# A planned order instead of a hand-timed one: linear attention into a causal gated unit on one core

## The chip, the core and the metric

The kernel runs on one core of a Trainium2 chip. A core has a matrix engine (TensorE, PE in the profile; its weight loads are listed as PEld), VectorE (DVE), ScalarE (ACT), GpSimd (POOL) and SyncE (SP), which here only issues transfers. Each engine has its own queue of instructions; engines wait for each other by semaphores. The metric is the device time of one launch in microseconds. Before the change the median of three runs is 404.75 us (404.43 to 405.25). The profiled execution has a span of 405.2 us.

## What is computed

```python
# q, k, v: (8, 8, 576, 64): batch, heads, sequence, head width
kv  = einsum('bhsd,bhse->bhde', k, v)
out = einsum('bhsd,bhde->bhse', q, kv)
rms = sqrt(mean(out * out, axis=-1, keepdims=True) + 1e-06)
x   = out / rms * g_norm                  # then (B, H, S, D) -> (B, S, H*D) = (8, 576, 512)
gate_pre = sum over 5 taps of conv_w[tap] * x shifted causally by tap   # depthwise, along the sequence
gate = sigmoid(gate_pre)
val  = x @ w_val                          # w_val, w_out: (512, 512)
out  = (gate * val) @ w_out
```

The three weights of the second half (`w_val`, `conv_w`, `w_out`) arrive as 64-bit floats and are narrowed to 32 bits on the chip, in eight steps per 128-column or 128-row piece: five on VectorE and three on ScalarE.

## The kernel before

For each of the eight batches: `kv_product` (four calls, one for each pair of heads), `kv_copy`, `turn_q` (VectorE) or, in batches 0 and 1, `turn_q_rows` (TensorE, then copies on ScalarE), and then for five chunks of the sequence, last chunk first, the chain below. `ps("raw")` has two PSUM buffers, `ps("tp")` two, `ps("mm")` three.

```python
    def raw_product(b, c):     # TensorE: raw = q @ kv, 4 matmuls into "raw" ("mm" for some of batch 0)
    def square(b, c):          # ScalarE: sq = raw ** 2
    def sums(b, c, pair, n):   # VectorE: ss = sum over the head
    def powers(b, pair, m, n): # GpSimd: rt = ss ** -0.5; from batch 2 on mostly two chunks in one instruction
        nc.gpsimd.tensor_tensor(
            out=st["rts", b, pair][0:m, 0:n, :], in0=st["ss", b, pair][0:m, 0:n, :],
            in1=mhalf[0:m, 0:n, :], op=ALU.pow)
    def normalise(b, c):       # VectorE: x = raw * rt; frees the "raw" buffer
    def turn_x(b, c):          # TensorE: 4 transposes of x into "tp"
    def keep_x(b, c):          # ScalarE: xT = turned x * g
    def halo(b):               # GpSimd: 4 small copies, once for each batch
```

Then for each of four 128-column tiles `jt` the gate and the value, and after a batch's eight gated halves the output product:

```python
    def gate_start(b, jt):       # ScalarE: first tap
    def gate_tap(b, jt, tap):    # VectorE: four more taps, one instruction each
    def gate_end(b, jt):         # ScalarE: sigmoid
    def val_product(b, jt, n):   # TensorE: 4 matmuls of 128x288 into "mm"; n is the half of the sequence
    def gated(b, jt, n):         # VectorE: gv = val * gate; frees the "mm" buffer
    def out_product(i, c):       # TensorE: 4 matmuls of 128x512 into "mm"
    def store(i, c):             # ScalarE copies "mm" to SBUF, SyncE issues four transfers
```

The order in which all these steps go into the engines' queues is a plan by hand: each step is entered with a nominal time, and the steps are emitted sorted by it.

```python
    plan = []

    def at(when, step, *args):
        plan.append((when, len(plan), step, args))
    ...
    attention(0, 17.0, 1.9, 7.0, 14.0)
    narrow_all(("wval", 0), 16.0, 0.5)
    narrow_all(("wval", 1), 20.2, 1.0)
    gate(0, 0, 32.0, 0.8)
    ...
    products(0, begin, 3.4)
    attention(1, 41.0, 2.2, 34.0, 38.0)
    begin += NK * NV * 3.4
    for jt in range(NK):
        gate(1, jt, begin + 0.2 + 4.0 * jt, 0.8)
        at(16.0 + 2 * jt, stage_weight, "wout", jt)
        narrow_all(("wout", jt), begin + 1.0 + 4.6 * jt, 0.57)
    for b in range(1, B):
        products(b, begin, DV)
        begin += NK * NV * DV
        outputs(b - 1, begin)
        ...
            attention(b + 1, first, 3.0, first - 8.0, first - 7.0)
    outputs(B - 1, begin)

    with tc.manual_schedule():
        for _, _, step, args in sorted(plan, key=lambda p: p[0:2]):
            step(*args)
```

Of the kernel before, what the change touches and what calls it, by code (L numbers as in the profile page):

```python
# [15 lines left out]
P = 128  # L16
EPS = 1e-6


@with_exitstack  # L20
def kernel(
# [56 lines left out]
    def ps(kind, shape, name):  # L78
        return psum.tile(shape, FP32, tag=kind, bufs=BANKS[kind], name=name)

    plan = []

    def at(when, step, *args):
        plan.append((when, len(plan), step, args))
# [6 lines left out]
    mhalf = const.tile([P, 2, H], FP32, name="mhalf")  # L91
# [32 lines left out]
    def load_kv(b, i):  # L124

        for name, src in (("k", k), ("v", v)):
            t = loads.tile([P, H // 2, NJ, D], FP32, tag=f"{name}{i}", name=f"{name}{i}_{b}")
            nc.sync.dma_start(
                out=t[:].rearrange("p h j d -> p h (j d)"),
                in_=src[b, i * H // 2:(i + 1) * H // 2, 0:SF, :].rearrange(  # L130
                    "h (p j) d -> p h (j d)", j=NJ),
            )
            st[name, b, i] = t
        if i == 0:
            for n, src in enumerate((k, v)):
                nc.sync.dma_start(
                    out=tails[b % 2][n][0:T], in_=src[b, :, SF:S, :].rearrange("h s d -> s h d"))
# [15 lines left out]
    def load_q_rows(b):  # L153

        for i in range(3):
            t = loads.tile([P, NB, D], FP32, tag="q", bufs=4, name=f"q{b}_{i}")
            t = t[:].rearrange("p n d -> p (n d)")
            if i < 2:
                t = t[:, 0:H // 2 * NJ * D]
                nc.sync.dma_start(  # L160
                    out=t.rearrange("p (h a) -> p h a", h=H // 2),
                    in_=q[b, i * H // 2:(i + 1) * H // 2, 0:SF, :].rearrange(
                        "h (p j) d -> p h (j d)", j=NJ),
                )
                st["q", b, i] = t.rearrange("p (h j d) -> p h j d", h=H // 2, j=NJ)
            else:
                t = t[0:T, 0:C].rearrange("p (h d) -> p h d", h=H)
                nc.sync.dma_start(out=t, in_=q[b, :, SF:S, :].rearrange("h s d -> s h d"))
                st["q", b, i] = t
# [74 lines left out]
    def turn_cw():  # L244

        nc.vector.tensor_scalar_mul(gcol[:], gcol[:], math.sqrt(D))
        cwps = ps("tp", [P, K, NK], "cwps")
        nc.tensor.transpose(
            cwps[:].rearrange("p k o -> p (k o)"), cw[:], ident[0:NK * K, 0:NK * K])
        nc.vector.tensor_copy(cwT[:], cwps[:])  # L250
# [32 lines left out]
    def turn_q_rows(b, j):  # L283
# [3 lines left out]
        for hp in range(HP):  # L287
            for r in range(2):
                half, h = divmod(2 * hp + r, H // 2)
                nc.tensor.matmul(  # L290
                    pq[r * D:(r + 1) * D, hp, 0:m],
                    st["q", b, half][:, h, j, :] if j < NJ else st["q", b, 2][:, 2 * hp + r, :],
                    ident[0:m, 0:m], start=True, stop=True)
        to = new_qT(b)[:].rearrange("p h (n t) -> p h n t", t=TB)
# [41 lines left out]
    def sums(b, c, pair, n):  # L336
        m = size(c)
        if n == 0:
            for kind in ("ss", "rts"):
                st[kind, b, pair] = work.tile([P, 2, H], FP32, tag=kind, bufs=3, name=f"{kind}{b}_{pair}")  # L340
        nc.vector.reduce_sum(out=st["ss", b, pair][0:m, n, :], in_=st["sq", b, c][0:m], axis=AX.X)  # L341
        st["rt", b, c] = st["rts", b, pair][:, n, :]

    def powers(b, pair, m, n):
        nc.gpsimd.tensor_tensor(  # L345
            out=st["rts", b, pair][0:m, 0:n, :], in0=st["ss", b, pair][0:m, 0:n, :],
            in1=mhalf[0:m, 0:n, :], op=ALU.pow)
# [78 lines left out]
    def store(i, c):  # L426
        ot = work.tile([P, C], FP32, tag="ot", bufs=3, name=f"ot{i}_{c}")
        nc.scalar.copy(out=ot[:], in_=st["po", i, c][:])  # L428
        for j in range(HB):
            bb, n = divmod(c * HB + j, NB)  # L430
            nc.sync.dma_start(  # L431
                out=rows_out[2 * i + bb, n], in_=ot[j * TB:(j + 1) * TB, :])

    ORDER = [NJ] + list(range(NJ - 1, -1, -1))
    TAPS = range(K - 2, -1, -1)

    def attention(b, first, step, kv_first, turn_first):

        for hp in range(HP):
            at(kv_first + 1.5 * hp, kv_product, b, hp)  # L440
            if b >= TURNED:
                at(turn_first + 1.5 * hp, turn_q, b, hp)
        at(kv_first + 1.5 * HP, kv_copy, b)
        for n, c in enumerate(ORDER):
            if b < TURNED:
                at(turn_first + 0.6 * n, turn_q_rows, b, c)
                t, pair, member, members = first + n * step, n, 0, 1
            else:
                pair, member = divmod(n + 1, 2)
                t, members = first + (0.0, 3.0, 4.5, 9.5, 11.0)[n], 2 if n else 1  # L450
                member = member if n else 0
            at(t, raw_product, b, c)
            at(t + 0.8, square, b, c)
            at(t + 1.5, sums, b, c, pair, member)
            if member == members - 1:
                at(t + 1.6, powers, b, pair, size(c), members)
            t += 1.5 * (members - 1 - member)
            at(t + 4.5, normalise, b, c)
            at(t + 6.5, turn_x, b, c)
            at(t + 7.0, keep_x, b, c)  # L460
            if n == 1:
                at(t + 7.8, halo, b)

    gate_done = {}

    def gate(b, jt, t, step, tap_step=gate_tap):
        at(t, gate_start, b, jt)
        for n, tap in enumerate(TAPS):
            at(t + (n + 1) * step, tap_step, b, jt, tap)
        gate_done[b, jt] = t + K * step + 0.3  # L470
        at(gate_done[b, jt], gate_end, b, jt)

    DV, DO = 2.5, 4.45

    def products(b, first, step):
        for jt in range(NK):
            for n in range(NV):
                t = first + (NV * jt + n) * step
                at(t, val_product, b, jt, n)
                at(max(t + DV, gate_done[b, jt] + 0.1), gated, b, jt, n)  # L480

    def outputs(b, first):

        for n, c in enumerate(range(NJ + 1) if b % 2 == 0 else range(NJ + 1, 2 * NJ + 1)):
            t = first + n * DO
            at(t, out_product, b // 2, c)
            at(t + DO, store, b // 2, c)


    at(0.0, stage_weight, "cw", 0)  # L490
    at(0.0, set_up)
    for i in range(2):
        at(0.1, load_kv, 0, i)
    at(0.2, load_q_rows, 0)
    for jt in range(NK):
        at(0.3, stage_weight, "wval", jt)
    for i in range(2):
        at(0.4, load_kv, 1, i)
    at(15.0, load_q_rows, 1)

    def narrow_all(key, first, step):
        for n in range(8):
            at(first + n * step, narrow_weight, *key, n)

    narrow_all(("cw", 0), 3.0, 0.2)
    at(4.9, turn_cw)
    attention(0, 17.0, 1.9, 7.0, 14.0)
    narrow_all(("wval", 0), 16.0, 0.5)
    narrow_all(("wval", 1), 20.2, 1.0)
    gate(0, 0, 32.0, 0.8)  # L510
    narrow_all(("wval", 2), 35.8, 0.5)
    gate(0, 1, 39.0, 0.8)
    narrow_all(("wval", 3), 43.0, 0.5)
    gate(0, 2, 47.0, 0.8)
    gate(0, 3, 51.0, 0.8)
    begin = 32.0
    products(0, begin, 3.4)
    attention(1, 41.0, 2.2, 34.0, 38.0)
    begin += NK * NV * 3.4
    for jt in range(NK):  # L520
        gate(1, jt, begin + 0.2 + 4.0 * jt, 0.8)
        at(16.0 + 2 * jt, stage_weight, "wout", jt)
        narrow_all(("wout", jt), begin + 1.0 + 4.6 * jt, 0.57)
    for b in range(1, B):
        products(b, begin, DV)
        begin += NK * NV * DV
        outputs(b - 1, begin)
        begin += (NJ + b % 2) * DO
        if b + 1 < B:
            first = begin - (28.0 if b == 1 else 34.0)  # L530
            for i in range(2):
                at(first - 28.0, load_kv, b + 1, i)
            for hp in range(HP):
                at(first - 27.0 + 0.1 * hp, load_q, b + 1, hp)
            attention(b + 1, first, 3.0, first - 8.0, first - 7.0)
            for jt in range(NK):
                gate(b + 1, jt, first + 20.5 + 6.5 * jt, 1.5)
    outputs(B - 1, begin)

    with tc.manual_schedule():  # L540
        for _, _, step, args in sorted(plan, key=lambda p: p[0:2]):
            step(*args)
# [30 lines left out]
```

## Time and profile before

| | value | from |
|---|---|---|
| time, median of 3 | 404.75 us | the runs |
| span of the profiled execution | 405.2 us | the page's head |
| TensorE busy | 358.5 us, 88% | part 1 of the page |
| VectorE busy | 216.8 us, 53% | part 1 |
| ScalarE busy | 142.4 us, 35% | part 1 |
| GpSimd busy | 78.8 us, 19% | part 1 |
| moved by DMA | 49.02 MB, mean 121 GB/s | part 2 |
| TensorE clock granted, mean | 0.965 | the list of cores |

How to read it: an engine's busy share is an average over the whole span. Part 2 of the page cuts the span in 40 slices of about 10.1 us and gives each engine's busy share in tenths; the row PEclk gives the granted TensorE clock in the same way. The idle time of an engine is listed with what released it. The timeline gives single instructions with their start. All durations of one instruction below are from the timeline or from the page's part 5.

### The profile page before, as it was taken

What the parts mean: (1) busy time and instruction counts of PE and PEld (TensorE: products, weight loads), DVE (VectorE), ACT (ScalarE), POOL (GpSimd) and SP (SyncE); (2) the same over time, 40 slices, a digit from 0 to 9 for tenths busy, and PEclk for the clock granted to TensorE, in tenths of its full rate; (3) what the DMA queues carried; (4) which work ended last, traced back from release to release, by engine and by line L of the source; (5) the groups of instructions that cost most, each with busy time, mean ns of one, the idle gap of its engine ahead of it and who ended that gap; (6) DMA issues with size and microseconds to landing.
All of it is one profiled execution on the core that took longest, in us unless ns stands there. A gap on an engine that the chain in (4) does not pass through costs nothing.

```text
span 405.2 us, 5563 instructions
## 1 busy us (share of the span) xinstructions
PE 358.5 (88%) x2081; PEld 239.6 (59%) x2081; DVE 216.8 (53%) x363; ACT 142.4 (35%) x253; POOL 78.8 (19%) x70
## 2 busy tenths in 40 slices
PE   1676996787669899999999999999999989999995
PEld 1664775665535477647764577557754766476442
DVE  3037646779952556767544756485539563761000
ACT  2166553453532324253134333341235322420111
POOL 2017004400042105400241024101430143000000
PEclk9995798999699899999999999999999999999999
DMA  7997014989401179326932495039713100310233
GB/s 186 320 295 213 3 53 145 231 243 233 122 0 47 39 174 256 77 53 172 248 94 53 91 298 152 20 92 268 186 26 78 28 2 0 79 28 5 74 76 78
DMA packets 42937, 49.02 MB, mean 121 GB/s; under 512 B 14218, under 2 KB 34718, under 8 KB 42910
## 3 DMA queue, kind: packets, MB, share of 16 engines
q1 hardware_dynamic: 42750, 48.67, 46.3%
q8 instruction: 16, 0.26, 0.3%
q14 instruction: 11, 0.09, 0.1%
q10 hardware_dynamic: 160, 0.00, 0.0%
HBM read 39.21 MB, written 9.44 MB: 120 GB/s over the span
## 4 chain that ended last, share of the span: by engine, by line
PE 60%; DVE 10%; POOL 7%; DMA 7%; ACT 7%; SPq 5%; issue 3%; POOLq 0%; DVEq 0%; ACTq 0%
PE out L420 22%; PE val L401 20%; PE raw L321 8%; POOL rts L345 7%; PE kv L260 4%; PE xTps L364 3%; DMA out_dram<-ot 3%; DVE x L352 3%; PE qTps L290 2%; SPq L431 2%; DVE ss L341 2%; DMA q<-in_q_dram 2%; ACT sq L331 2%; DMA vl<-in_v_dram 2%; DVE gate L389 1%
## 5 line engine op out<-in xcount | busy, mean ns | idle before, releaser
L401 PE MATMUL val<-xT,wval 128*128 128x288 f32 x512 | 140.6, 424 | 1.9 <-ACT xT L371 1.6
L420 PE MATMUL out<-wout,gv 128*128 128x512 f32 x288 | 127.4, 597 | 0.0
L389 DVE SCALAR_TENSOR_TENSOR gate<-xT,cwT,gate 128x576 f32<-128x576 f32 x128 | 102.5, 808 | 29.3 <-ACT gate L383 27.7
L401 PEld LDWEIGHTS val<-xT,wval 128*128 128x128 f32 x512 | 96.7, 196 | 30.2 <-issue 3.0
L345 POOL TENSOR_TENSOR rts<-ss,mhalf 128x16 f32<-128x16 f32 (+2 forms) x28 | 67.9, 2427 | 237.4 <-DVE ss L341 237.4
L420 PEld LDWEIGHTS out<-wout,gv 128*128 128x128 f32 x288 | 54.4, 192 | 63.0 <-issue 62.5
L321 PE MATMUL raw<-kvbd,qT 128*128 128x128 f32 (+1 forms) x320 | 44.9, 286 | 18.8 <-DVE x L352 12.0
L321 PEld LDWEIGHTS raw<-kvbd,qT 128*128 128x128 f32 (+1 forms) x320 | 39.7, 185 | 27.4 <-issue 11.4
L341 DVE TENSOR_REDUCE ss<-sq 128x8 f32<-128x520 f32 (+1 forms) x40 | 27.5, 689 | 35.3 <-ACT sq L331 35.2
L331 ACT ACTIVATE sq<-raw 128x512 f32<-128x512 f32 (+1 forms) x40 | 23.6, 593 | 63.0 <-PE raw L321 62.8
L410 DVE TENSOR_TENSOR gv<-val,gate 128x288 f32<-128x288 f32 x64 | 28.7, 452 | 30.3 <-PE val L401 28.1
L428 ACT COPY ot<-out 128x512 f32<-128x512 f32 x36 | 21.0, 582 | 65.3 <-DMA out_dram<-ot 27.2
L352 DVE TENSOR_TENSOR x<-raw,rts 128x512 f32<-128x512 f32 (+1 forms) x40 | 26.4, 684 | 31.8 <-POOL rts L345 31.8
L371 ACT ACTIVATE xT<-xTps,gcol 128x512 f32<-128x512 f32 (+1 forms) x40 | 24.5, 642 | 53.2 <-PE xTps L364 53.2
L364 PE MATMUL xTps<-ident,x 128*128 128x128 f32 (+1 forms) x160 | 23.5, 284 | 9.6 <-DVE x L352 9.2
L364 PEld LDWEIGHTS xTps<-ident,x 128*128 128x128 f32 (+1 forms) x160 | 18.5, 149 | 19.0 <-issue 12.9
L396 ACT ACTIVATE gate<-gate 128x576 f32<-128x576 f32 x32 | 21.8, 682 | 18.3 <-DVE gate L389 18.2
L260 PEld LDWEIGHTS kv<-v,k 128*64 128x64 f32 x512 | 19.5, 150 | 10.8 <-issue 9.3
L260 PE MATMUL kv<-v,k 128*64 128x64 f32 x512 | 22.6, 239 | 3.2 <-DMA v<-in_v_dram 3.2
L383 ACT ACTIVATE gate<-xT,cwT 128x576 f32<-128x576 f32 x32 | 24.7, 772 | 0.2
L278 DVE STREAM_TRANSPOSE qT<-q 128x576 f32<-128x576 f32 x24 | 18.5, 770 | 0.0
L270 ACT COPY kvbd<-kv 64x256 f32<-64x256 f32 x16 | 5.9, 366 | 31.1 <-PE kv L260 31.0
(52 smaller groups left out, 106.0 us busy)
## 6 DMA issues: line engine op xcount, KB each, us to landing
q<-in_q_dram SPq DMA_DIRECT2D x96, 140.0 KB, 4.3
out_dram<-ot SPq DMA_DIRECT2D x144, 64.0 KB, 1.7
k<-in_k_dram SPq DMA_DIRECT2D x16, 512.0 KB, 6.0
v<-in_v_dram SPq DMA_DIRECT2D x16, 512.0 KB, 8.3
q<-in_q_dram SPq DMA_DIRECT2D x4, 512.0 KB, 8.2
w_wval<-in_moe_w_val_dram SPq DMA_DIRECT2D x4, 512.0 KB, 8.5
w_wout<-in_moe_w_out_dram SPq DMA_DIRECT2D x4, 512.0 KB, 3.2
kl<-in_k_dram SPq DMA_DIRECT2D x8, 128.0 KB, 6.9
```

Source lines behind the costliest of these rows:

```text
L260: nc.tensor.matmul(kvp[r * D:(r + 1) * D, hp, :], st["k", b, half][:, h, j, :] if j < NJ else kl[:, 2 * hp + r, :], st["v", b, half][:, h, ...
L321: nc.tensor.matmul(raw[0:m, hp * P:(hp + 1) * P], st["qT", b][:, hp, c * P:c * P + m], kv_bd[b % 2][:, hp, :], start=True, stop=True,)
L331: nc.scalar.activation(out=sq[0:m, :, 0:D], in_=st["raw", b, c][0:m].rearrange("p (h e) -> p h e", h=H), func=AF.Square,)
L341: nc.vector.reduce_sum(out=st["ss", b, pair][0:m, n, :], in_=st["sq", b, c][0:m], axis=AX.X)
L345: nc.gpsimd.tensor_tensor(out=st["rts", b, pair][0:m, 0:n, :], in0=st["ss", b, pair][0:m, 0:n, :], in1=mhalf[0:m, 0:n, :], op=ALU.pow)
L352: nc.vector.tensor_tensor(out=x[0:m].rearrange("p (h e) -> p h e", h=H), in0=st["raw", b, c][0:m].rearrange("p (h e) -> p h e", h=H), in1= ...
L364: nc.tensor.transpose(px[:, kc, 0:m], st["x", b, c][0:m, kc * P:(kc + 1) * P], ident[0:m, 0:m])
L383: nc.scalar.activation(out=gate[:], in_=xTs[b % 3][:, jt, HALO:SX], func=AF.Copy, scale=cwT[:, K - 1, jt:jt + 1])
L389: nc.vector.scalar_tensor_tensor(out=gate[:], in0=xTs[b % 3][:, jt, tap * TB:tap * TB + S], scalar=cwT[:, tap, jt:jt + 1], in1=gate[:], op ...
L401: nc.tensor.matmul(val[:], wval[:, kc, jt * P:(jt + 1) * P], xTs[b % 3][:, kc, HALO + n * SV:HALO + (n + 1) * SV], start=(kc == 0), stop=( ...
L410: nc.vector.tensor_tensor(out=gv[:, jt, first:first + SV], in0=st["val", b, jt, n][:], in1=st["gate", b, jt][:, n * SV:(n + 1) * SV], op=A ...
L420: nc.tensor.matmul(po[:], gv[:, jt, c * P:(c + 1) * P], wout[:, jt, :], start=(jt == 0), stop=(jt == NK - 1),)
```

## The change

The nominal times stay, but no longer fix the order alone. Each step is now entered in a `Planner` with its engine, a duration, what it needs, what it gives, and which buffers it takes and frees. The planner walks through time: among the steps whose needs and buffers are there it takes the one that can start first on its engine (ties go to the earlier nominal time), not more than `ahead` microseconds before its nominal time, and so finds the order of all steps. The instructions themselves stay the same except in three places: the power on GpSimd is taken for every chunk alone, the two-chunk form is gone; the eight value products of a batch go second half of the sequence first (a product now needs only the chunks of its half); and a few steps are split so that each part can be placed by itself (the copy of an output and its stores, the matmuls and the copies of `turn_q_rows`, each load).

```diff
+class Planner:
+    HOP = 0.15
+    LANDING = 1.9
+    def add(self, engine, time, want, fn, *args, needs=(), gives=(), takes=(), frees=(), load=0.0, ahead=12.0):
+    ...
+    def order(self):
+        free, transfers, left, found = {}, 0.0, list(self.steps), []
+        while left:
+            best = None
+            for step in left:
+                t = self.ready(step)
+                if t is None:
+                    continue
+                now = free.get(step["engine"], 0.0)
+                key = (max(t, now), step["want"], step["at"])
+                if best is None or key < best[0]:
+                    best = key, step
+    ...
-    def powers(b, pair, m, n):
+    def powers(b, c):
+        m = size(c)
+        rt = work.tile([P, H], FP32, tag="rt", bufs=3, name=f"rt{b}_{c}")
         nc.gpsimd.tensor_tensor(
-            out=st["rts", b, pair][0:m, 0:n, :], in0=st["ss", b, pair][0:m, 0:n, :],
-            in1=mhalf[0:m, 0:n, :], op=ALU.pow)
+            out=rt[0:m], in0=st["ss", b, c][0:m], in1=mhalf[0:m], op=ALU.pow)
     ...
     def products(b, first, step):
         for jt in range(NK):
-            for n in range(NV):
+            for n in range(NV - 1, -1, -1):
     ...
-    for jt in range(NK):
-        at(0.3, stage_weight, "wval", jt)
-    for i in range(2):
-        at(0.4, load_kv, 1, i)
-    at(15.0, load_q_rows, 1)
     ...
+    loads_kv(0, 0.1)
+    loads_q(0, 0.2)
+    for jt in range(NK):
+        weight(("wval", jt), 0.3 + 0.01 * jt, 16.0 + (4.0, 8.0, 20.0, 28.0)[jt], 0.5)
+    loads_kv(1, 0.4)
+    loads_q(1, 0.5)
     ...
     with tc.manual_schedule():
-        for _, _, step, args in sorted(plan, key=lambda p: p[0:2]):
-            step(*args)
+        set_up()
+        for step in plan.order():
+            step["fn"](*step["args"])
```

What this does to the queues, from the two programs:

- SyncE: three small loads of batch 0's and 1's `q` are reordered (the tail rows first). `k`, `v` and `q` of batch 2 are issued after two of the four `w_out` pieces instead of after all four. From batch 4 on, loads stand among the stores of outputs instead of in front of them.
- TensorE, batches 0 and 1: three of batch 1's `kv_product` calls and one value product of batch 0 move ahead of the last transposes of batch 0's `x`; all five `raw_product` calls of batch 0 stand together; batch 2's `kv_product` calls stand in front of and among the `raw_product` calls of batch 1, and batch 3's among the value products of batch 1.
- VectorE, batches 0 and 1: each four steps of a weight's narrowing stand close together; one `w_out` piece and two `turn_q` of batch 2 move ahead of the last `normalise` of batch 1; the rest of `w_out` stands between the gate taps of batch 1.
- GpSimd: 40 powers of one chunk instead of 28 instructions of one or two chunks. In batch 0 `halo` stands in front of the last chunk's power instead of after it.
- From batch 3 on the TensorE order is nearly that of before, apart from the halves and single places.

## The prediction

> **What bounds the kernel now.** I read the page's slices first, then the busy time by stage, then who makes TensorE wait, and last the timeline of single engines. In the slices each digit is a busy share in tenths, and PEclk is the granted clock.
>
> ```profile
> PE   1676996787669899999999999999999989999995
> ...
> DVE  3037646779952556767544756485539563761000
> ...
> PEclk9995798999699899999999999999999999999999
> ```
>
> From about slice 15 (143 us) TensorE shows 9 at full clock to the end. In front of that it has holes, and after each its clock is low for a while. I cut the span at landmarks of the program: 31.3 is the first transpose of x in batch 0, 82.0 the end of the last `normalise` of batch 1, 117.0 the last `gated` of batch 1, 143.4 the end of batch 0's fifth output product, 354.2 the first value product of batch 7. The columns are the stretch, its length, busy us (and count) of PE, PEld, DVE, ACT and POOL, then clock, DMA share and GB/s.
>
> ```profile
> 31.30:82.00 50.70, 41.15 (x308) 31.17 (x308) 33.55 (x53) 25.29 (x49) 17.47 (x17) 0.83 0.46 124
> 82.00:117.00 35.00, 26.14 (x173) 19.63 (x174) 30.69 (x54) 16.66 (x27) 1.63 (x1) 0.90 0.65 171
> 117.00:143.40 26.40, 23.09 (x77) 11.65 (x75) 10.88 (x17) 8.09 (x14) 6.79 (x6) 0.94 0.16 41
> 143.40:354.20 210.80, 205.78 (x1198) 137.22 (x1198) 125.44 (x192) 73.11 (x124) 48.00 (x35) 1.00 0.46 117
> 354.20:405.20 51.00, 46.38 (x136) 25.46 (x134) 8.08 (x14) 8.46 (x14) 0.00 (x0) 0.99 0.21 52
> ```
>
> The two last stretches are TensorE work, 98% and 91% (the rest of the last is the final copy and store). An order can gain nothing there. In the three first ones TensorE is idle 9.6 + 8.9 + 3.3 = 21.8 us, and its clock is 0.83, 0.90 and 0.94: 0.17 x 41 + 0.10 x 26 + 0.06 x 23, some 11 us more if all the clock came back. So the prize is at most 33 us of 405, all before 143 us. Between 82 and 117 us it is VectorE that is full: 30.7 of 35 us. What TensorE waits for from 31 to 145 us:
>
> ```profile
> PE xTps L364 <- DVE x L352: 9.2, 6, 3.1
> PE raw L321 <- DVE x L352: 7.0, 4, 3.1
> PE raw L321 <- ACT kvbd L270: 5.5, 1, 5.5
> ```
>
> 16.2 us are waits for `normalise`, the end of the chain square, sums, power, normalise, behind other work in VectorE's queue. The 5.5 us is one wait at 104.7 us: batch 2's `kv_copy` stood behind a `w_out` narrowing in ScalarE's queue, and that waited for VectorE:
>
> ```profile
> 101.16 0.72 ACT L204 ACTIVATE wexp_wout<-wexp_wout,biases 128x512 uint32<-128x512 uint32 x1 [4.76 <-DVE wexp_wout L199]
> ...
> 103.96 0.73 ACT L270 COPY kvbd<-kv 64x256 f32<-64x256 f32 x2
> ```
>
> **What the skill says.** "PSUM — Partial Sum Buffer", section "Engine vs sequencer instructions": the queues of ScalarE, VectorE and GpSimd are strict first in, first out, and matmuls keep program order. The trace agrees: `kv_copy` sat behind a 4.76 us wait that was not its own. So an order can cost or save time with the same instructions. "TensorE: Matmul & The Clock Gate", section "What's actually happening": after an idle window of about 3.4 us the array runs at half clock until it has been busy again. The trace shows that kind of thing: after the 5.47 us hole at 104.7 us two value products take 4.08 us instead of 3.88 and the `raw_product` 1.97 instead of about 1.05. Filling holes should give back clock too. I take no more than half of the 11 us.
>
> **The change, stage by stage.** I follow the changed queues by hand with durations of the trace. Back to back on VectorE one gate tap takes 0.73 us (start to start), sums or normalise 0.60, gated 0.37, transpose of q 0.70, a weight's four later steps 2.25 together, the first 0.35. On TensorE a value product takes 2.1, a `raw_product` 0.9, a turn of x 0.45, a pair of heads of kv 0.7 to 1.0, an output product 3.43.
>
> 1. *To 31.3 us: nothing.* This is loading: TensorE starts turning q at 17.05 us on its last transfer. The small q load in front lets 0.7 us of TensorE work begin earlier, but the large loads end when they did. Batch 0's last `normalise`: here I expect a loss of about 1 us. The power chain on GpSimd is full from 30.8 to 38.1 us, and `halo` (0.98 us) now stands in front of the last power instead of after it. It started at 38.14 before, now about 39.
>
> 2. *31.3 to batch 1's last normalise.* Three kv calls (3 us at the slow clock) and a value product (2.1) of TensorE move into the hole before batch 0's last turn. From there VectorE has, by the new queue, 16 taps (11.7), 8 gated (3.0), 10 sums and normalise (6.0), two weights of w_val and one of w_out with two first steps (7.4), two transposes (1.4): 29.5 us. It cannot run full: batch 1's raw products need the ScalarE copies of turned q, which I find at about 54 us, so `raw_product` comes at 56 to 57 us as before (57.66), and from there the five-link chain runs through two raw buffers, about 4 us a link pair. I find some 6.5 us of waits: 39.5 + 29.5 + 6.5, about 76 us, against 82.0. **Gain 6.**
>
> 3. *To batch 1's last gated.* VectorE's queue then holds 16 taps (11.7), 8 gated (3.0), three weights of w_out with two first steps (7.4), three transposes (2.1), two sums and one normalise (1.8): 26 us. 4.4 us of the old stage (one weight, one first step, two transposes: 2.25 + 0.7 + 1.4) has been done in stage 2, where VectorE was idle for a third of the time. TensorE will stand for some 4 us, as three "mm" buffers wait for the gates, and 3 us for the first normalise of batch 2; VectorE is the bound here and hides it. kv and q of batch 2 are loaded by then: their issue moves from 65.7 us (behind the last w_out piece) to the thirties, so the 5.5 us wait is gone. With 1.5 us of waits: 76 + 27.5 = 103.5 against 117.0. **Gain 13.5 in all.**
>
> 4. *To the end of batch 0's outputs.* TensorE then has five outputs (17.2), two raw (1.8), four turns (1.8): 20.8 us, where the old stage took 26.4. Its two-chunk powers of 2.9 us, with waits of 3.1 us for normalise, become powers of 1.65 to 1.95. Moreover batch 3's kv (2.6 us) is already done, which stood at 143.4 before. With 1.5 us of waits: about 126, against 143.4 + 2.6 = 146. **Gain 20.**
>
> 5. *The rest: nothing either way.* TensorE had 5.0 us idle in 210.8. The single powers shorten the chain by a microsecond, reversed halves let value products start before the last chunk is kept, and gates stand farther ahead. GpSimd goes from 67.9 us of powers to about 40 x 1.85 = 74, far from a bound. The tail is nine outputs of 3.43 and a store, unchanged.
>
> The sum is 20 us by a walk that takes every hand-over as on time. I take off 3 to 4 us for what a walk by hand misses: hand-overs between engines, and the half clock after two holes in stage 3. That gives 404.75 - 17.5, about **387 us**.
>
> **The rivals.**
>
> *VectorE takes over as the bound and keeps the gain.* From 39.5 us to the last gated there are 29.5 + 26 = 55.5 us of VectorE work in 64 us by my walk, 87% full, and one late semaphore stops everything behind it. At 78% the same work takes 71 us and ends 7 us later: 394. For it: stage 3 was already 88% full. Against it: 9.93 busy us between 90 and 100 us show that it can run full where its inputs are ready.
>
> *A new wait in the steady state.* Eight value products go in a new order through three buffers, and turned x follows its raw product after only two value products and one raw (5.1 us) against a chain of square 0.6, sums 0.7, power 1.7, normalise 0.7 and hand-overs, about 4.2 us. A queue delay of 1 us on VectorE would stall TensorE. One to two us in each of six batches make 6 to 12 us: 393 to 399. Against it: the old order had the same slack in front of its third raw product and lost 5.0 us in 210 us.
>
> *The holes were hidden anyway.* If the loads set the first stages the order cannot help. Against it: the DMA share is 0.46 in stage 2 and at 0.01 between 40 and 50 us. This would leave 402 to 405.
>
> **Range and chances.** A full success with clock regained would be about 380; the two first rivals together 397. I give 379 to 397 eight chances in ten. The 2% line is 404.75 x 0.98 = 396.65: faster 0.84, within 2% 0.12, slower 0.04, the last for a queue that blocks in a place that I did not see.
>
> **What would show it.** Batch 1's last normalise should end near 76 us, its last gated near 104, batch 0's fifth output near 126, and the 5.5 us wait for `kvbd` be gone; VectorE should be 90% busy from 76 to 104 us. From batch 2's values on TensorE should stay above 97%, and the time from there to the end be 259 us as before (405.2 - 146). If those last 259 us grow, the second rival is right; if the landmarks come late with VectorE full, the first; if TensorE's waits are for loads, the third. The prediction is wrong if ScalarE's queue, which I followed least closely, holds back the copies of turned q or the first gates.

## The result, and the profile after

The changed kernel takes 375.93 us (median of 4 runs, 374.06 to 377.53) against 404.59 us: ratio 0.929, 95% interval 0.924 to 0.934. It is 28.7 us faster, and lies below the predicted range of 379 to 397. Two of its runs can differ by 3 us, so the intervals here are about 2 us wide to each side, and smaller differences between versions are not settled below.

First the slices of the changed kernel, in tenths busy (one slice is now 9.3 us), with the granted clock.

```profile
PE   1787999949799999999999899999999999999995
...
DVE  3057989999933995957329754955339644920000
...
PEclk9998999989999999999999999999999999999999
```

TensorE had holes from the second to the fourteenth slice. Behind the loading (the first four slices) two are left now, the ninth slice and, smaller, the eleventh. VectorE stands at 9 in the five slices from the seventh to the eleventh, which take in both. Now the same five stages by landmarks (first turn of x, batch 1's last normalise, its last gated, batch 0's fifth output, batch 7's first value product, end); columns as before.

```profile
29.10:71.30 42.20, 40.11 (x394) 32.71 (x395) 36.74 (x61) 27.25 (x53) 17.12 (x17) 0.96 0.93 258
71.30:99.40 28.10, 20.84 (x165) 16.02 (x164) 26.67 (x46) 12.48 (x20) 2.40 (x2) 0.94 0.26 79
99.40:120.10 20.70, 20.70 (x75) 10.99 (x74) 8.30 (x13) 8.91 (x15) 7.38 (x8) 1.00 0.52 141
120.10:322.30 202.20, 201.00 (x1118) 134.38 (x1117) 131.06 (x196) 74.19 (x123) 46.92 (x45) 1.00 0.40 112
322.30:373.40 51.10, 46.50 (x137) 25.57 (x135) 7.85 (x14) 7.24 (x12) 0.00 (x0) 1.00 0.20 52
```

TensorE is idle 2.1 us in the first of them instead of 9.6, 7.3 in the second, not at all in the third, and 1.2 in the long fourth. VectorE is busy 26.7 of 28.1 us in the second. Who makes TensorE wait from 31 to 145 us in the changed kernel (total us, times, longest):

```profile
PE val L476 <- DVE gv L485: 5.7, 2, 5.1
PE xTps L439 <- DVE x L427: 3.3, 2, 2.1
PE val L476 <- ACT xT L446: 0.4, 1, 0.4
```

The wait of 5.5 us for `kvbd` and the 7.0 us of raw products waiting for normalise are gone. A new wait of 5.1 us has come: a value product of batch 1 for a free "mm" buffer, that is for the gates on VectorE.

The two profiled spans differ by 405.2 - 373.4 = 31.8 us, 3 more than the medians. A span is 1.8 us less than the time of its launch; so the profiled launch before took about 407 us, 2.4 above its median, and the one after 375.2, 0.7 below its own. Landmarks below are from the profiles, times of versions are medians.

### The profile page after: what moved, and what is told of

Its sections match the earlier page's. It is cut to its first block, busy times and chain, and to the rows that moved or that the text cites. A ratio compares the mean times of both kernels' runs of the same rounds, so it can differ in the third digit from the quotient of the medians.

```text
span 373.4 us, 5575 instructions
## 1 busy us (share of the span) xinstructions
PE 345.3 (92%) x2081; PEld 234.2 (63%) x2081; DVE 220.5 (59%) x363; ACT 142.9 (38%) x253; POOL 79.3 (21%) x82
## 4 chain that ended last, share of the span: by engine, by line
PE 71%; DVE 9%; DMA 8%; SPq 4%; ACT 3%; POOL 2%; issue 2%; DVEq 0%; ACTq 0%; POOLq 0%
PE val L476 28%; PE out L495 24%; PE raw L396 8%; PE kv L330 5%; PE xTps L439 4%; DVE gate L464 3%; DMA out_dram<-ot 3%; SPq L510 3%; DMA q<-in_q_dram 3%; DMA v<-in_v_dram 2%; PE qTps L360 2%; POOL rt L420 2%; ACT ot L503 2%; DVE gv L485 1%; DVE x L427 1%
## 5 line engine op out<-in xcount | busy, mean ns | idle before, releaser
L476 PE MATMUL val<-xT,wval 128*128 128x288 f32 x512 | 135.7, 413 | 6.1 <-DVE gv L485 5.7
L464 DVE SCALAR_TENSOR_TENSOR gate<-xT,cwT,gate 128x576 f32<-128x576 f32 x128 | 102.8, 816 | 30.2 <-ACT gate L458 27.6
L420 POOL TENSOR_TENSOR rt<-ss,mhalf 128x8 f32<-128x8 f32 (+1 forms) x40 | 68.7, 1722 | 227.3 <-DVE ss L414 227.3
L476 PEld LDWEIGHTS val<-xT,wval 128*128 128x128 f32 x512 | 94.7, 192 | 32.6 <-DVE gv L485 6.1
L495 PEld LDWEIGHTS out<-wout,gv 128*128 128x128 f32 x288 | 53.6, 190 | 61.0 <-issue 60.7
L396 PE MATMUL raw<-kvbd,qT 128*128 128x128 f32 (+1 forms) x320 | 42.8, 279 | 0.5 <-ACT qT L386 0.5
L396 PEld LDWEIGHTS raw<-kvbd,qT 128*128 128x128 f32 (+1 forms) x320 | 38.5, 180 | 5.9 <-issue 3.1
L446 ACT ACTIVATE xT<-xTps,gcol 128x512 f32<-128x512 f32 (+1 forms) x40 | 25.6, 645 | 40.7 <-PE xTps L439 40.7
L427 DVE TENSOR_TENSOR x<-raw,rt 128x512 f32<-128x512 f32 (+1 forms) x40 | 27.4, 684 | 21.3 <-POOL rt L420 21.0
L406 ACT ACTIVATE sq<-raw 128x512 f32<-128x512 f32 (+1 forms) x40 | 23.8, 595 | 39.5 <-PE raw L396 38.0
L471 ACT ACTIVATE gate<-gate 128x576 f32<-128x576 f32 x32 | 21.8, 682 | 35.9 <-DVE gate L464 35.7
L458 ACT ACTIVATE gate<-xT,cwT 128x576 f32<-128x576 f32 x32 | 22.3, 764 | 0.3
```

The lines of the kernel that those rows point to most:

```text
L396: nc.tensor.matmul(raw[0:m, hp * P:(hp + 1) * P], st["qT", b][:, hp, c * P:c * P + m], kv_bd[b % 2][:, hp, :], start=True, stop=True,)
L420: nc.gpsimd.tensor_tensor(out=rt[0:m], in0=st["ss", b, c][0:m], in1=mhalf[0:m], op=ALU.pow)
L427: nc.vector.tensor_tensor(out=x[0:m].rearrange("p (h e) -> p h e", h=H), in0=st["raw", b, c][0:m].rearrange("p (h e) -> p h e", h=H), in1= ...
L446: nc.scalar.activation(out=xTs[b % 3][:, :, first:first + m], in_=st["px", b, c][:, :, 0:m], func=AF.Copy, scale=gcol[:],)
L464: nc.vector.scalar_tensor_tensor(out=gate[:], in0=xTs[b % 3][:, jt, tap * TB:tap * TB + S], scalar=cwT[:, tap, jt:jt + 1], in1=gate[:], op ...
L476: nc.tensor.matmul(val[:], wval[:, kc, jt * P:(jt + 1) * P], xTs[b % 3][:, kc, HALO + n * SV:HALO + (n + 1) * SV], start=(kc == 0), stop=( ...
```

## The experiments

**The single power alone.** In the plan by hand, every chunk gets its own power; the `normalise`, turn and copy of a chunk that used to wait for its pair are entered 1.5 us earlier with it.

```diff
-                pair, member = divmod(n + 1, 2)
-                t, members = first + (0.0, 3.0, 4.5, 9.5, 11.0)[n], 2 if n else 1
-                member = member if n else 0
+                t, pair, member, members = first + (0.0, 3.0, 4.5, 9.5, 11.0)[n], n, 0, 1
-            t += 1.5 * (members - 1 - member)
```

> The kernel before, with the power on GpSimd for every chunk alone from batch 2 on too (no two-chunk form), each normalise at the nominal time of its own chunk; all else as before. Theory A (the single power removes the waits of the steady part): the 5.0 us that TensorE waits for normalise after 143 us go, and about 2 of the 3.3 us before it: 404.6 - 7 = 397 to 399 us. Theory B (those waits went because of the order of the value products and of VectorE's queue, not because of the power): 403 to 405 us.

Measured: 396.44 us, ratio to before 0.979 (0.975 to 0.982). Theory A, a little stronger. In the steady part TensorE's waits before the edit, after 143.4 us, are

```profile
PE raw L321 <- DVE x L352: 5.0, 7, 1.3
```

and after it, from 143.4 to 345 us,

```profile
PE raw L321 <- DVE x L352: 0.4, 2, 0.2
```

So this edit is worth 8 us when made alone. By the profiles 5.7 us of its gain lie behind batch 0's fifth output (256.1 us from there to the end instead of 261.8), the rest just in front of it.

**The two-chunk power put back.** In the changed kernel, sums of two chunks go into one tile and one power follows, with 2.95 us for it in the plan.

```diff
+    def pairing(b, c):
+        n = [NJ, 3, 2, 1, 0].index(c)
+        if b < TURNED or n == 0:
+            return n, 0, 1
+        return (n + 1) // 2, (n + 1) % 2, 2
     ...
+            if member == members - 1:
+                keys = [(b, cc) for cc in (ORDER[n - members + 1:n + 1])]
+                plan.add(
+                    "POOL", 1.75 if members == 1 else 2.95, t + 2.3, powers, b, c,
     ...
```

> The changed kernel with the two-chunk power put back from batch 2 on (1.75 us for one chunk, 2.95 us for two in the planner); all else planned as in the changed kernel. Theory A (single power): TensorE waits for normalise again once or twice for each of six batches, about 1 us each: 376 + 5 = 380 to 383 us. Theory B (order): 375 to 377 us.

Measured: 377.43 us, 0.932 (0.928 to 0.937); against the changed kernel's 0.929 not told apart. Theory B in the time: the same pair that costs 8 us in the hand order costs 1.5 here, which the intervals do not tell from nothing. The trace shows why. TensorE in batch 2 (start, length; `x8` is one value product, since each matmul of the program stands as two in the profile):

```profile
134.12 1.16 PE L396 MATMUL raw<-kvbd,qT 128*128 128x128 f32 x8
135.12 7.93 PE L485 MATMUL val<-xT,wval 128*128 128x288 f32 x32
142.88 0.60 PE L448 MATMUL xTps<-ident,x 128*128 128x128 f32 x4
```

The planner, told of the longer power, put four value products in a row in front of the next turn, where the changed kernel has two. No wait for normalise is left in its steady part (120 to 330 us). The single power and the new order are two cures of one wait, so their gains do not add.

**The small load first.** One line of the kernel before.

```diff
-        for i in range(3):
+        for i in (2, 0, 1):
```

> The kernel before with one edit: batch 0's and 1's small q load goes in front of the two large ones. Theory A (the first turn of q waited only for the small load, which came last): TensorE starts to turn q at about 15.5 instead of 17.05 us, and all of it carries to the first raw product at 22.2 to 22.5 us instead of 24.23; the hand plan then loses a part behind the weights: 402.5 to 404. Theory B (the large loads set the turning): the first raw product stays at 24 us and the time at 404 to 405.

Measured: 402.49 us, 0.993 (0.992 to 0.995), 2.2 us. Theory A: turning of q begins at 15.51 us and ends at 21.2 instead of 23.7. Before, and with the edit:

```profile
17.05 6.66 PE L290 MATMUL qTps<-ident,q 64*64 64x64 f32 x80 [2.00 <-DMA q<-in_q_dram]
```

```profile
15.51 5.67 PE L290 MATMUL qTps<-ident,q 64*64 64x64 f32 x80
```

The large loads, then, had landed in time; before, the turning waited for the small one, which was issued last. In the first 30 us of the kernel before, loads of 512 KB land a median of 8.2 to 8.8 us after their issue, those of 128 KB 8.5 to 8.8 us.

**One wrong number in the planner.** It takes three buffers for incoming weights, the pool has four.

```diff
-"w64": 3
+"w64": 4
```

> The changed kernel with one number of the planner corrected: four buffers for weights on their way in instead of three, as the pool really has. The fourth w_val piece is then loaded in front of batch 1's k and v, and the wait of 2.33 us of VectorE for it, at 36.8 us, goes. Theory A (from there VectorE is the bound, so its wait carries): 373.5 to 374.5 us. Theory B (TensorE had other work until 37.96 us, and k and v of batch 1 come later): 375.5 to 378 us.

Measured: 376.75 us, 0.929 (0.924 to 0.934). The wait it was aimed at, in the changed kernel,

```profile
36.77 0.45 DVE L267 TENSOR_SCALAR wexp_wval<-w_wval 128x512 uint32<-128x512 uint32 x1 [2.33 <-DMA w_wval<-in_moe_w_val_dram]
```

is gone from VectorE's list, and no gain is seen. Theory B fits; the upper edge of A, 374.5 us, is just inside the interval. The trace shows other waits in its place:

```profile
35.97 0.69 DVE L427 TENSOR_TENSOR x<-raw,rt 128x512 f32<-128x512 f32 x1 [1.18 <-POOL rt L420]
38.07 0.69 DVE L279 SCALAR_TENSOR_TENSOR wexp_wval<-w_wval,wexp_wval 128x512 uint32<-128x512 uint32 x1 [1.41 <-ACT wexp_wval L276]
```

The gate taps behind them begin at 40.82 us, in the changed kernel at 40.20.

**Halves, running ahead, durations, early loads.** Four edits of the changed kernel, each made alone and each undoing one thing the planner was given.

```diff
# old halves
-            for n in range(NV - 1, -1, -1):
+            for n in range(NV):
-                    needs=[("xT", b, c) for c in HALVES[n]] + [("wval", jt)],
+                    needs=[("xT", b, c) for c in ORDER] + [("wval", jt)],
# no running ahead
-    def add(..., load=0.0, ahead=12.0):
+    def add(..., load=0.0, ahead=0.0):
# flat times
-            end = start + step["time"]
+            end = start + {"PE": 1.5, "DVE": 0.75, "ACT": 0.75, "POOL": 1.5, "SP": 1.5}[step["engine"]]
# late loads of batch 2
-            loads_kv(b + 1, first - 28.0)
-            loads_q(b + 1, first - 27.0)
+            loads_kv(b + 1, first - 28.0 if b > 1 else 66.0)
+            loads_q(b + 1, first - 27.0 if b > 1 else 66.5)
```

> The changed kernel with the value products first half of the sequence first, each waiting for all chunks of x as before the change. Theory A (the halves are a small part: one value product of 2.1 us no longer fills the hole in front of batch 0's last turn, and the same for batch 1): 377 to 379.5 us. Theory B (the halves carry the steady part): TensorE waits come back after 120 us, 380 to 383 us. Theory C (nothing): 375 to 377 us.

> The changed kernel with `ahead` 0 instead of 12: no step may start before its nominal time, so what is left of the planner is that a step not yet ready lets another go first. Batch 2's kv and the first w_out piece then stand behind batch 1's raw products again. Theory A (running ahead fills the early holes and is most of the gain): 384 to 392 us. Theory B (letting ready steps go first is most of it; the nominal times only break ties): 376 to 380 us.

> The changed kernel with one duration for each engine in the planner (TensorE, GpSimd and transfers 1.5 us, VectorE and ScalarE 0.75) instead of one for each step. Theory A (the walk's durations matter, since each queue is strictly in order and a wrong guess blocks it): 382 to 390 us. Theory B (needs and buffers matter, durations little): 376 to 380 us.

> The changed kernel with batch 2's k, v and q not loaded before 66 us of the plan, as before the change (65.7 us). Theory A (early loads let 1 us of batch 2's kv and two transposes of q fill idle time before 71 us; without them VectorE has 1.4 us more to do in its full stage): 377 to 379 us. Theory B (they carry the gain of the early part, and the 5.5 us wait comes back): 381 to 386 us. Theory C (planned around): 375 to 377 us.

Measured: 377.03 (ratio 0.931, 0.925 to 0.937), 377.02 (0.930, 0.927 to 0.934), 375.83 (0.927, 0.923 to 0.930) and 376.18 us (0.928, 0.924 to 0.932). None differs from the changed kernel by more than the intervals allow. The theories that gave an edit much weight (380 us and more) are out; a loss of 1 or 2 us, as theory A has it for the halves, is not told from nothing. Flat durations and no running ahead each leave the gain whole. What all four keep is the rule that a step which is not ready lets a ready one go first; that this rule makes the gain is inferred from what is left, no run takes it away by itself.

**The hand order put back, engine by engine.** The planner's walk is kept, but on a chosen engine only the next step of the hand plan's list may start. All four runs use old halves, so their base is 377.03 us, and they keep single powers. There is no run with ScalarE alone or with VectorE: while TensorE is planned freely, ScalarE's hand order leaves the walk with no step that can start.

```diff
+                line = self.fixed.get(step["engine"])
+                if line and line[0] is not step:
+                    continue
     ...
+    plan.fixed = {e: sorted((s for s in plan.steps if s["engine"] == e),
+                            key=lambda s: ranks[(s["fn"].__name__,) + s["args"]]) for e in HAND}
```

> The changed kernel with old halves (377.0 us), in which VectorE alone keeps the order of the plan by hand; the planner places the steps of all other engines around it, with single powers and its own order of loads. Theory A (the hand order of VectorE, with its weights spread between gate taps and normalise, was the cost): 388 to 394 us. Theory B (the cost lay in TensorE's and ScalarE's order): 377 to 381 us.  Theory C (each order is good only with the others, so the cost comes back in part whichever is put back): 383 to 388 us.

> The same, with TensorE alone in the order of the plan by hand. Theory A (VectorE's order was the cost): 377 to 381 us. Theory B (TensorE's order, with batch 1's kv after batch 0's turns and batch 2's kv after batch 1's raw products): 386 to 394 us. Theory C (in part): 382 to 386 us.

> The same, with TensorE, VectorE and ScalarE all in the order of the plan by hand, with single powers; of the planner only the order of the loads (and GpSimd's, nearly the same) is left. Against the kernel before with single powers (396.4 us) it has the small q load first and batch 2's loads early. If the order of those three engines is the rest of the gain: 392 to 396 us. If the loads are: 377 to 385 us.

> The same, with TensorE and ScalarE in the order of the plan by hand and VectorE planned. Theory A (VectorE's order was the cost): 378 to 383 us. Theory B (the two others): 388 to 394 us. Theory C (in part, so that it takes all three together to lose the whole): 383 to 388 us.

| hand order on | us | ratio to before (interval) | above 377.03 |
|---|---|---|---|
| none | 377.03 | 0.931 (0.925 to 0.937) | |
| VectorE | 387.14 | 0.959 (0.954 to 0.964) | 10.1 |
| TensorE | 384.29 | 0.948 (0.942 to 0.953) | 7.3 |
| TensorE, ScalarE | 386.13 | 0.955 (0.953 to 0.957) | 9.1 |
| all three | 396.43 | 0.980 (0.977 to 0.982) | 19.4 |

The base and each row are known to about 2 us. Within that the two halves add up: 10.1 + 9.1 = 19.2 against 19.4. With all three back the time is that of the single power in the plan by hand (396.44).

That does not make the order of the loads worthless. In the run with all three, the small load still comes first, and batch 0's first raw product starts at 22.37 us (24.09 with the single power alone). But the run also keeps GpSimd's new order: `halo`, 2.04 us here, stands in front of batch 0's last power, VectorE waits 1.78 us for it, and the last `normalise` starts at 37.74 instead of 37.99. So a gain and a loss nearly cancel there.

VectorE's own waits, from 22 us to batch 1's last gated, show where it lost time. The three longest with all three by hand (the last gated ends at 115.9 us):

```profile
DVE wexp_wval L284 <- ACT wexp_wval L281: 7.9, 2, 6.2
DVE ss L419 <- ACT sq L411: 7.9, 5, 2.8
DVE gate L469 <- ACT gate L463: 5.9, 3, 2.8
```

The changed kernel (99.4 us):

```profile
DVE wexp_wval L267 <- DMA w_wval<-in_moe_w_val_dram: 2.3, 1, 2.3
DVE wexp_wval L279 <- ACT wexp_wval L276: 1.6, 1, 1.6
DVE gv L485 <- PE val L476: 1.1, 2, 0.7
DVE ss L414 <- ACT sq L406: 1.0, 1, 1.0
```

With the shorter waits the lists come to 27.6 and 7.3 us: 20.3 us less waiting, and the last gated 16.5 us earlier. The window matters. To 145 us the first list has 16.1 us for squares, but half of it lies behind the last gated; from 117 to 143.4 us TensorE is busy for 26.25 of 26.4 us, so VectorE's waits there cost next to nothing.

**Which steps.** As with VectorE by hand, but the weights are free; as with TensorE by hand, but kv is free.

```diff
-                if line and line[0] is not step:
+                if line and line[0] is not step and step["fn"].__name__ != "narrow_weight":
# in the other run: "kv_product"
```

> As the run with VectorE alone in the hand order (387.1 us), but the narrowing of weights is free: the planner puts those steps where it likes among the others, which keep the hand order. Theory A (the fixed places of the weights were the cost): 377 to 380 us. Theory B (the places of sums, normalise and gate taps against each other): 384 to 388 us. In between, 381 to 383, both.

> As the run with TensorE alone in the hand order (384.3 us), but kv_product is free. Theory A (kv of batches 1 and 2 at fixed late places was the cost): 377 to 380 us. Theory B (the places of value products, turns and raw products): 382 to 385 us.

Measured: 380.59 us (0.940, 0.937 to 0.943), between theory A and "both": the weights' places were 6.5 of VectorE's 10.1 us. And 378.34 us (0.935, 0.931 to 0.940), theory A: the places of kv were 6 of TensorE's 7.3. VectorE's waits go the same way: to batch 1's last gated they are 21.5 us with VectorE by hand (it ends at 109.5), 12.0 with the weights free (102.7) and 8.8 with no hand order and old halves (99.8).

**Is VectorE the bound that is left?** Two edits of the changed kernel. In one batch 2's q goes through TensorE and ScalarE, so that VectorE has four transposes less; in the other it does them twice.

```diff
# less
-    TURNED = 2
+    TURNED = 3
# more
-        nc.vector.transpose(out=new_qT(b)[:, hp, :], in_=st["q", b, hp][:, :, 0:TB])
+        for _ in range(2 if b == 2 else 1):
+            nc.vector.transpose(out=new_qT(b)[:, hp, :], in_=st["q", b, hp][:, :, 0:TB])
```

> The changed kernel with batch 2's q turned on TensorE with ScalarE's copies, as batches 0 and 1 are, instead of by four transposes on VectorE: 2.8 us less for VectorE between 69 and 90 us, some 2.5 us more for TensorE and 4 more for ScalarE there. Theory A (VectorE is the bound of the stretch from 37 to 99 us): 372.5 to 374.5 us. Theory B (the turns get in the way of TensorE and of ScalarE's gates): 376 to 380 us.

> The changed kernel with each of batch 2's four VectorE transposes of q done twice (the same data again), and so told to the planner: 2.8 us more of VectorE work between 69 and 90 us, nothing else. Theory A (VectorE is the bound there): 378 to 379.5 us. Theory B (TensorE's stalls of 5.1 and 2.1 us there have slack): 375.5 to 377 us.

Measured: 371.86 us, 0.918 (0.916 to 0.921), with an interval below that of the changed kernel (0.924 to 0.934); and 379.33 us, 0.936 (0.932 to 0.939). So 2.8 us less gave 4.1, and 2.8 us more cost 3.4: theory A both times. The cost is only just clear of the noise, since single runs of the two kernels overlap. The edit to "less" also loads batch 2's q in other pieces; but no wait of VectorE for q stands between 37 and 100 us in either kernel. From 60 to 100 us the changed kernel has

```profile
60.00:100.00 40.00, 32.34 (x226) 25.47 (x227) 37.88 (x64) 21.47 (x35) 9.56 (x9) 0.96 0.43 122
```

and the one with fewer transposes

```profile
60.00:100.00 40.00, 38.51 (x323) 29.92 (x320) 37.14 (x63) 24.90 (x49) 11.19 (x10) 1.00 0.45 124
```

In it TensorE is nearly full as well (38.5 us), the clock is back at 1.00, and the wait of 5.1 us for a gate is 0.5. That may be why it gains more than the 2.8 us taken off VectorE; it was not tried apart. This version beats both kernels.

## Why the prediction was wrong

The mechanism was right: waits in strictly ordered queues, gone by another order, with VectorE as the next bound. What failed is step 5, "the rest: nothing either way", which measured 5.9 us, and next to it the waits charged in step 2, 6.5 us where there were 2.0. By the prediction's own steps, in the profiles:

| step | predicted | measured |
|---|---|---|
| 1: first raw product of batch 0 | 24.2 | 22.2 |
| 1: batch 0's last normalise ends | 39.5 | 37.8 |
| 2: batch 1's last normalise ends | 76 | 71.3 |
| 3: batch 1's last gated ends | 103.5 | 99.4 |
| 4: batch 0's fifth output ends | 126 | 120.1 |
| 5: gain from there to the end | 0 | 5.9 |

*Step 1, wrong by 2 us.* "The large loads end when they did" did not matter: it was the small load that the turning of q waited for, and the run with this load first shows 2.2 us for that line alone in the hand order. The loss of 1 us to `halo` does exist (1.78 us of wait with all three engines by hand), but in the changed kernel it is hidden: the last power ends at 35.9 us, and VectorE stands until 36.77 for a piece of `w_val`.

*Step 2, wrong by 3 more.* I charged 6.5 us of waits to VectorE and put the first raw product of batch 1 "at 56 to 57 us as before". From 37.8 to 71.3 us VectorE waited only 2.0 us (its work was about 2 us longer than my sum):

```profile
DVE ss L414 <- ACT sq L406: 1.0, 1, 1.0
DVE x L427 <- POOL rt L420: 0.6, 3, 0.2
DVE gv L485 <- PE qTps L360: 0.4, 1, 0.4
```

The raw product came at 52.85 us, since ScalarE's last copy of turned q ended at 51.0 and not "at about 54":

```profile
50.81 0.17 ACT L389 COPY qT<-qTps 128x8 f32<-128x8 f32 x1
52.85 2.18 PE L396 MATMUL raw<-kvbd,qT 128*64 128x128 f32 x16
```

TensorE stands still only 2.1 us in this stage. That the kv calls that moved forward did this is likely, not shown for this stage alone: freeing kv in TensorE's hand order gave back 6 us of the whole kernel.

*Step 3, right.* 27.5 us predicted, 28.1 measured, VectorE 95% busy. That VectorE is the bound and TensorE's stalls lie behind it is shown by the pair of transposes, less and more. The stall for "mm" buffers was predicted at 4 us and measured at 5.1, and the one for normalise at 3 and measured at 2.1. (The 0.7 us that this step writes for one first step of a weight is that of two; it is not in its sum.)

*Step 4, 1.8 us too long.* I added 1.5 us of waits to 20.8 us of work; the stage took 20.7.

*Step 5, the largest error: "nothing either way".* The prediction took the 5.0 us that TensorE was idle in 210.8 us as a floor ("An order can gain nothing there"). It was one wait, seven times, for a `normalise` behind the two-chunk power, and I had written in the same paragraph that the single power shortens that chain. The term is 5.9 us of the 11.8 that the walk was short in the profiles. In the hand plan the single power is the cure (8 us with stage 4's part); in the planned order the order alone is one as well, as the two-chunk power put back shows.

*The clock.* The prediction read "two value products take 4.08 us instead of 3.88" after the hole before. It was one, `x8`:

```profile
106.64 4.08 PE L401 MATMUL val<-xT,wval 128*128 128x288 f32 x8
80.31 3.63 PE L476 MATMUL val<-xT,wval 128*128 128x288 f32 x8 [5.13 <-DVE gv L485]
```

Against the usual 2.1 us it ran at about half speed, and so did most of the one behind the new hole of 5.1 us. A hole thus cost more clock than I thought; in the sum this stood only in the reserve.

*The reserve.* The text takes off 3 to 4 us for hand-overs and its sum takes off 2.5. None was needed: stages 3 and 4 came out at 28.1 and 20.7 us against 27.5 and 22.5 without it.

The rivals: no new wait came in the steady state (1.2 us in all), VectorE did become the bound but did not keep the gain, and loads set only step 1. What I said of ScalarE's queue as the danger did not happen.

What stays open: a part of VectorE's 10.1 us, 3.6, is in the places of sums, normalise and taps and was not taken apart further. ScalarE's own part, 1.8 us with TensorE's order in place, is within the intervals.

## What to carry to other kernels

In strictly ordered queues, count what each engine waits for at the head of its queue, up to the landmark where it stops being the bound; here VectorE's list (27.6 us by hand, 7.3 after) told more than the busy shares did. Waits behind that landmark do not count. To find an order, a walk in which a step that is not ready lets another go first was enough: taken one at a time, neither its durations nor its running ahead mattered. And an idle time in a "full" stage is not a floor: 5 us in 210 came from one repeated wait, and two independent edits could each take it away.

## What the runs showed of the hardware

That a load of 128 KB (rows of 256 bytes) issued last takes as long as loads of 512 KB issued before it: 8.7 us from issue to landing for the small one, a median of 8.2 for the large ones of q, and 2.2 us of the whole kernel in the hand order for its place in the queue. And that TensorE is slow behind a long hole: behind holes of 3.06 and 5.47 us in the kernel before and of 5.13 us in the changed one, the first value product took 3.77, 4.08 and 3.63 us, where 2.1 is usual.
